# Where the conversion of the weights stands between softmax steps, and who swaps the halves of x: one start-up, two arrangements

## The chip, the core and the metric

The kernel runs on one core of a Trainium2 chip. The time is device microseconds from the first to the last instruction of the program on that core; the median of three runs is taken. The engines meant below are TensorE (PE in the profile, its weight loads PEld), VectorE (DVE), ScalarE (ACT), GpSimd (POOL, "Pool" in the text) and SyncE (SP), which here only issues transfers.

## The reference

Attention with a threshold, then a bilinear feed-forward network on its output. q, k and v have 8 batches, 8 heads, 576 rows and 64 columns, in float32; the three weights have 512 x 1536, 512 x 1536 and 1536 x 512 elements, in float64.

```python
scores = scale * np.matmul(q, k.transpose(0, 1, 3, 2))
thresh = np.max(scores, axis=-1, keepdims=True) - tau
scores = np.where(scores >= thresh, scores, -1000000000.0)
scores = scores - np.max(scores, axis=-1, keepdims=True)
attn = np.exp(scores)
attn = attn / (np.sum(attn, axis=-1, keepdims=True) + 1e-09)
attn_out = np.matmul(attn, v)
# bridge: (B,H,S,D) -> (B*S, H*D), 4608 x 512
x = attn_out.transpose(0, 2, 1, 3).reshape(B * S, H * D)
out = ((x @ w_a) * (x @ w_b)) @ w_out
```

## The kernel before

The attention goes by **units**: a pair of heads and 128 queries (units 0 to 3 of a pair), or the last 64 queries of both heads (unit 4, the *tail*). A unit's scores fill four 64 x 64 quadrants of TensorE, in float32. The feed-forward network goes by **blocks** of 256 rows of x; its steps are put between the units' steps by a budget of columns (`advance`), so that TensorE always has work once x and the weights are there. In the first units neither is there: x comes from the attention, and the weights come as float64 and are put together from their two 32-bit words by five small steps on three engines, one piece of 128 x 512 at a time, 36 pieces in all.

```python
def load_weights(limit, engine=nc.sync):
    while len(raws) < limit and state["loaded"] < NPIECES:
        n = state["loaded"]
        raw = work.tile([P, CW, 2], U32, tag="xT", bufs=XT_BUFS, name="raw")
        ...                                    # one or two transfers, 512 KB
        raws[n] = raw
        state["loaded"] = n + 1

def convert_first(n):                          # ScalarE, twice
    raw, top = raws[n], pieces[n][0]
    low = work.tile([P, CW], FP32, tag="osb", bufs=OSB_BUFS, name="low")
    nc.scalar.activation(top, raw[:, :, 1].bitcast(FP32), AF.Abs)
    nc.scalar.activation(low, raw[:, :, 0], AF.Copy, bias=2.0, scale=2.0 ** -51)
    stages[n] = low

def convert_clamp(n):                          # Pool
    nc.gpsimd.tensor_scalar(top, top, ..., op0=ALU.min, op1=ALU.max)

def convert_sign(n):                           # VectorE; gives the raw slot free
    nc.vector.scalar_tensor_tensor(out=low, in0=hi, scalar=0x80000000, in1=low,
                                   op0=ALU.bitwise_and, op1=ALU.bitwise_or)

def convert_shift(n):                          # VectorE
    nc.vector.tensor_scalar(top, top, 3, None, op0=ALU.logical_shift_left)

def convert_add(n):                            # Pool
    nc.gpsimd.tensor_tensor(top, top, low, op=ALU.add)
    state["converted"] = n + 1

def scores(i, u):
    ...
    for c in range(2):
        for t in range(n):                     # n = 2, in a tail 1
            for j in range(2):
                r = slice(j * D, (j + 1) * D)
                o = t if u < NT else 1 - j     # tails: crossed quadrants
                q0, to = (u * P + t * D if u < NT else MAIN), slice(o * D, (o + 1) * D)
                nc.tensor.matmul(sc[j if u < NT else 0][to, c], qT[r, q0:q0 + D],
                                 kT[r, c * SH:(c + 1) * SH], start=True, stop=True)
    ...                                        # VectorE: maxima; Pool: bias, threshold

def weigh(i, u):
    ...                                        # ScalarE: exponentials; VectorE: masks and sums

def turn_pe(i, u):                             # units 0 to 7: weights turned by TensorE
    tp = banks(512, "tp")
    ...                                        # 8 matmuls with diag(1 / sum)
    for j in range(2):
        nc.scalar.copy(wT[:, 5 * j:5 * j + NT], tp[:, j])
    tp = banks(P, "tp")[:, 0]
    ...                                        # 2 matmuls
    nc.scalar.copy(wT[:, NT], tp)

def exchange(x, xs, hp, c0, c1, engine):       # swaps the partition halves of x
    for r in range(2):
        engine.tensor_copy(xs[r * D:(r + 1) * D, hp, c0:c1], x[(1 - r) * D:(2 - r) * D, hp, c0:c1])

def weighted_unit(i, u):
    pv = product(turned.pop((i, u, "pe")), loaded[i]["v"], P)
    ...
    join(x_of[b, 0][:, hp, u * P:(u + 1) * P], pv[:, 0], pv[:, 1])
    exchange(x_of[b, 0], state["xs"], hp, u * P, (u + 1) * P, nc.vector)
    if hp == HP - 1:
        state["rows"] = u + 1
        if u == 0:
            blocks.append(((x_of[b, 0], state["xs"]), ("first", b, 0)))

def ffn(xT, what):
    n = CH // P                                # 2
    steps = [(f, 0, HALF) for f in range(NG * n)]
    if kind == "first":                        # the first block starts with half its rows
        steps = [(f, c, c + P) for c in (0, P) for f in range(n)] + steps[n:]
    ...
```

All PSUM tiles (scores, pv, tp, pab, po) come from one pool of four buffers of two banks each. Raw weights, x and xS share seven buffers. The loop over the units, cut to the conversion and the order around it (`of(g, False)` is the first piece of unit g, `of(g, True)` the others; units 0 to 3 have two pieces, 4 to 9 three, 10 to 14 two):

```python
for g in range(len(units) + PV_LAG):
    scores(i, u)
    ...
    if 2 <= g < BY_PE + 2:
        weighted_unit(*units[g - 2])
    for n in of(g - 1, False):
        convert_add(n)
    for n in of(g - 1, True):
        convert_clamp(n)
    if g < 3:
        prep_copy(*prep_pe(g + 1, "q"))        # VectorE: q and k of the next pair, turned
    for n in of(g - 1, True):
        convert_sign(n)
    load_weights(5 if g < 10 else 4)
    ...
    weigh(i, u)
    if 0 < g <= BY_PE:
        turn_pe(*units[g - 1])
    if g < 3:
        prep_copy(*prep_pe(g + 1, "k"))
    ...
    for n in of(g, False):
        convert_first(n)
        convert_clamp(n)
    reciprocal(i, u, ...)
    for n in of(g - 1, True):
        convert_shift(n)
    for n in of(g - 1, True):
        convert_add(n)
    ...                                        # diagonals or normalise, on ScalarE
    for n in of(g, False):
        convert_sign(n)
    load_weights(5 if g < 10 else 4)
    ...
    advance(...)                               # feed-forward steps
    for n in of(g, True):
        convert_first(n)
    for n in of(g, False):
        convert_shift(n)
    advance(PORTIONS[3] * pace)
```

Of the kernel before, what the change touches and what calls it, by code (L numbers as in the profile page):

```python
# [11 lines left out]
U32 = mybir.dt.uint32  # L12
# [38 lines left out]
def kernel(  # L51
# [11 lines left out]


# [118 lines left out]
    raws, stages = {}, {}  # L183
    state = {"loaded": 0, "converted": 0, "rows": 0}

    def load_weights(limit, engine=nc.sync):

        while len(raws) < limit and state["loaded"] < NPIECES:
            n = state["loaded"]
            raw = work.tile([P, CW, 2], U32, tag="xT", bufs=XT_BUFS, name="raw")  # L190
            src = pieces[n][1]
            for r, part in enumerate(src):
                dst = raw.rearrange("p f w -> p (f w)")[r * D:r * D + P // len(src)]
                if len(src) == 2:
                    dst = dst.rearrange("p (k f) -> p k f", k=2)
                engine.dma_start(dst, part)
            raws[n] = raw
            state["loaded"] = n + 1
# [37 lines left out]
    def convert_add(n):  # L236
        if n in stages:
            top, low = pieces[n][0].bitcast(I32), stages.pop(n).bitcast(I32)
            nc.gpsimd.tensor_tensor(top, top, low, op=ALU.add)
            state["converted"] = n + 1  # L240
# [4 lines left out]
    nc.sync.dma_start(tau_sb, tau.to_broadcast([P, 1]))  # L245
# [9 lines left out]
    load_rows(1, "k", rooms[3], nc.scalar)  # L255
    load_weights(2)
# [48 lines left out]
    def scores(i, u):  # L305
# [3 lines left out]
        for c in range(2):  # L309
            for t in range(n):  # L310
                for j in range(2):
                    r = slice(j * D, (j + 1) * D)
                    o = t if u < NT else 1 - j
                    q0, to = (u * P + t * D if u < NT else MAIN), slice(o * D, (o + 1) * D)
                    nc.tensor.matmul(sc[j if u < NT else 0][to, c], qT[r, q0:q0 + D],  # L315
                                     kT[r, c * SH:(c + 1) * SH], start=True, stop=True)
# [51 lines left out]
    def turn_pe(i, u):  # L368
# [16 lines left out]
        nc.scalar.copy(wT[:, NT], tp)  # L385
# [10 lines left out]
    def turn_blocks(i, u):  # L396
# [20 lines left out]
        else:  # L417
# [5 lines left out]
            for g in range(G):  # L423
                c = slice((1 - g // 2) * NB, (2 - g // 2) * NB)
                w0 = swap.shape[2] - TAIL + (g % 2) * Q
                nc.sync.dma_start(swap[c, :, w0:w0 + Q].rearrange("c p w -> p c w"),  # L426
                                  tb[g * Q:(g + 1) * Q])
# [43 lines left out]

    def weighted_unit(i, u):
# [7 lines left out]
        exchange(x_of[b, 0], state["xs"], hp, u * P, (u + 1) * P, nc.vector)  # L480
        if hp == HP - 1:
            state["rows"] = u + 1
            if u == 0:
                blocks.append(((x_of[b, 0], state["xs"]), ("first", b, 0)))
# [23 lines left out]
    def ffn(xT, what):  # L508
# [7 lines left out]
        if kind == "first":  # L516
            steps = [(f, c, c + P) for c in (0, P) for f in range(n)] + steps[n:]
# [115 lines left out]
    def of(g, late):  # L633

        return early.get(g, [])[1:] if late else early.get(g, [])[0:1]

    for g in range(len(units) + PV_LAG):
# [15 lines left out]
        for n in of(g - 1, False):  # L653
            convert_add(n)
        for n in of(g - 1, True):
            convert_clamp(n)
        if g < 3:
            prep_copy(*prep_pe(g + 1, "q"))
        for n in of(g - 1, True):
            convert_sign(n)  # L660
        load_weights(5 if g < 10 else 4)
# [21 lines left out]
        for n in of(g, False):  # L683
# [4 lines left out]
        for n in of(g - 1, True):  # L688
            convert_shift(n)
        for n in of(g - 1, True):  # L690
            convert_add(n)
# [4 lines left out]
        for n in of(g, False):  # L696
            convert_sign(n)
# [10 lines left out]
        for n in of(g, True):  # L708
            convert_first(n)
        for n in of(g, False):  # L710
            convert_shift(n)
# [38 lines left out]
```

## Time and profile before

| | before |
|---|---|
| median of 3 runs (lowest to highest) | 1526.21 us (1524.84 to 1528.06) |
| span of the profiled run, mean granted TensorE clock | 1524.0 us, 0.988 |
| busy: TensorE, weight loads | 1467.9 us (96%), 1145.1 us (75%) |
| busy: VectorE, ScalarE, Pool | 877.9 us (58%), 588.9 us (39%), 260.4 us (17%) |
| HBM read and written | 127.40 MB, 89.65 MB |
| raw weights | 36 pieces of 512 KB; median landing 4.2 to 5.4 us |

The page gives busy time as an average over the whole span, in which the first 165 us and the rest have different limits; so the views by stretches of time say more here. In the rows of groups the columns are: line, engine, operation, result<-inputs, shape, count | busy us, mean ns of one | idle time just before them, and what ended most of it. In the timeline they are: start, us, engine, line, operation, tiles, count, and in brackets the idle time before it and what ended it. TensorE shows two records for each float32 matmul.

### The profile page before, as it was taken

What the parts mean: (1) busy time and instruction counts of PE and PEld (TensorE: products, weight loads), DVE (VectorE), ACT (ScalarE), POOL (GpSimd) and SP (SyncE); (2) the same over time, 40 slices, a digit from 0 to 9 for tenths busy, and PEclk for the clock granted to TensorE, in tenths of its full rate; (3) what the DMA queues carried; (4) which work ended last, traced back from release to release, by engine and by line L of the source; (5) the groups of instructions that cost most, each with busy time, mean ns of one, the idle gap of its engine ahead of it and who ended that gap; (6) DMA issues with size and microseconds to landing.
All of it is one profiled execution on the core that took longest, in us unless ns stands there. A gap on an engine that the chain in (4) does not pass through costs nothing.

```text
span 1524.0 us, 51117 instructions
## 1 busy us (share of the span) xinstructions
PE 1467.9 (96%) x22640; PEld 1145.1 (75%) x22640; DVE 877.9 (58%) x1844; ACT 588.9 (39%) x935; POOL 260.4 (17%) x662
## 2 busy tenths in 40 slices
PE   5779999999999999999999999999999999999998
PEld 4567586786978587778877887778886978687775
DVE  4999677577756765665545755476655765610000
ACT  4667444344434443443333433344433443410000
POOL 2666311111110111121100101011110111110000
PEclk9889999999999999999999999999999999999999
DMA  9558888779867976796537966589648976530000
GB/s 196 134 154 210 184 149 204 167 165 189 202 150 160 188 188 134 157 184 153 138 93 143 194 147 144 115 180 186 154 112 162 189 175 128 127 79 15 2 16 15
DMA packets 624557, 220.38 MB, mean 145 GB/s; under 512 B 542928, under 2 KB 612048, under 8 KB 624336
## 3 DMA queue, kind: packets, MB, share of 16 engines
q1 hardware_dynamic: 621968, 216.52, 65.2%
q8 instruction: 178, 2.92, 0.8%
q10 hardware_dynamic: 2368, 0.59, 0.2%
q14 instruction: 43, 0.35, 0.1%
HBM read 127.40 MB, written 89.65 MB: 142 GB/s over the span
## 4 chain that ended last, share of the span: by engine, by line
PE 87%; DVE 6%; DMA 3%; SPq 1%; ACT 1%; issue 1%; POOL 0%; DVEq 0%; ACTq 0%; POOLq 0%
PE pab L533 45%; PE po L553 23%; PE pv L452 9%; PE sc L315 9%; DVE low L228 2%; DMA raw<-in_moe_w_a_dram 1%; DVE w L339 1%; DVE mx L322 1%; DVE tb L404 1%; DMA wT<-swap 0%; SPq L414 0%; SPq L426 0%; DVE wa_sb L234 0%; SPq L142 0%; DMA swap<-tb 0%
## 5 line engine op out<-in xcount | busy, mean ns | idle before, releaser
L553 PE MATMUL po<-wo_sb,h 64*64 64x512 f32 x3456 | 423.3, 590 | 0.0
L553 PEld LDWEIGHTS po<-wo_sb,h 64*64 64x64 f32 x3456 | 226.0, 133 | 130.3 <-issue 73.4
L322 DVE TENSOR_REDUCE mx<-sc 128x1 f32<-128x576 f32 x288 | 205.0, 749 | 201.6 <-PE sc L315 189.9
L335 ACT ACTIVATE w<-sc,bias,scalars 128x576 f32<-128x576 f32 x288 | 226.7, 827 | 188.7 <-POOL bias L323 180.9
L533 PE MATMUL pab<-xS,wa_sb 64*64 64x256 f32 (+1 forms) x3520 | 278.6, 373 | 3.3 <-POOL xS L462 3.3
L533 PE MATMUL pab<-xS,wb_sb 64*64 64x256 f32 (+1 forms) x3520 | 278.2, 375 | 0.5 <-issue 0.5
L315 PE MATMUL sc<-kT,qT 64*64 64x288 f32 x2304 | 254.4, 417 | 19.7 <-DVE w L339 8.4
L358 ACT ACTIVATE w<-w,rcp 128x576 f32<-128x576 f32 x272 | 197.7, 768 | 183.8 <-DVE rcp L352 183.7
L323 POOL TENSOR_SCALAR bias<-mx,scalars 128x1 f32<-128x1 f32 x288 | 84.8, 295 | 1032.0 <-DVE mx L322 617.4
L533 PE MATMUL pab<-xT,wb_sb 64*64 64x256 f32 (+1 forms) x3136 | 249.0, 374 | 1.7 <-DVE h L541 1.7
L533 PE MATMUL pab<-xT,wa_sb 64*64 64x256 f32 (+1 forms) x3136 | 246.2, 375 | 3.0 <-DVE xT L442 1.8
L339 DVE SCALAR_TENSOR_TENSOR w<-sc,thr,w 128x576 f32<-128x576 f32 x288 | 222.4, 804 | 18.7 <-ACT w L335 16.4
L533 PEld LDWEIGHTS pab<-xS,wa_sb 64*64 64x64 f32 x3520 | 193.5, 133 | 35.5 <-POOL xS L462 10.1
L533 PEld LDWEIGHTS pab<-xS,wb_sb 64*64 64x64 f32 x3520 | 197.0, 134 | 27.6 <-issue 1.1
L533 PEld LDWEIGHTS pab<-xT,wa_sb 64*64 64x64 f32 x3136 | 175.2, 134 | 28.9 <-DVE xT L442 2.1
L315 PEld LDWEIGHTS sc<-kT,qT 64*64 64x64 f32 x2304 | 148.0, 136 | 63.0 <-issue 20.1
L452 PE MATMUL pv<-wT,vm 64*64 64x320 f32 (+3 forms) x2592 | 192.8, 384 | 2.3 <-ACT h L539 1.4
L533 PEld LDWEIGHTS pab<-xT,wb_sb 64*64 64x64 f32 x3136 | 176.1, 134 | 24.2 <-DVE h L541 2.3
L404 DVE STREAM_TRANSPOSE tb<-w 128x576 f32<-128x576 f32 x240 | 171.4, 752 | 1.3 <-ACT w L358 1.3
L452 PEld LDWEIGHTS pv<-wT,vm 64*64 64x64 f32 x2592 | 149.2, 137 | 28.8 <-issue 8.1
L541 DVE TENSOR_TENSOR h<-h,pab 128x512 f32<-128x512 f32 (+1 forms) x110 | 72.8, 662 | 122.3 <-PE pab L533 121.7
L539 ACT COPY h<-pab 128x512 f32<-128x512 f32 (+1 forms) x110 | 63.1, 573 | 199.0 <-PE pab L533 198.5
(59 smaller groups left out, 744.4 us busy)
## 6 DMA issues: line engine op xcount, KB each, us to landing
swap<-tb SPq DMA_DIRECT2D x240, 288.0 KB, 5.3
wT<-swap SPq DMA_DIRECT2D x28, 1440.0 KB, 7.5
wT<-swap SPq DMA_DIRECT2D x32, 1152.0 KB, 6.3
vm<-in_v_dram SPq DMA_DIRECT2D x32, 288.0 KB, 4.9
swap<-tbt SPq DMA_DIRECT2D x128, 72.0 KB, 2.8
out_dram<-osb SPq DMA_DIRECT2D x32, 256.0 KB, 4.6
qm<-in_q_dram SPq DMA_DIRECT2D x112, 72.0 KB, 3.6
km<-in_k_dram SPq DMA_DIRECT2D x112, 72.0 KB, 4.8
```

Of the source, the lines that this page charges most:

```text
L315: nc.tensor.matmul(sc[j if u < NT else 0][to, c], qT[r, q0:q0 + D], kT[r, c * SH:(c + 1) * SH], start=True, stop=True)
L322: nc.vector.tensor_reduce(mx[:, c], sc[j], axis=AX.XY, op=ALU.max)
L323: nc.gpsimd.tensor_scalar(bias[:, c], mx[:, c], e_nscale, None, op0=ALU.mult)
L335: nc.scalar.activation(w.rearrange("p (c k) -> p c k", c=2), s, AF.Exp, bias=bias[:, j:j + 1], scale=e_scale)
L339: nc.vector.scalar_tensor_tensor(out=wv, in0=s, scalar=thr[:, j:j + 1], in1=wv, op0=ALU.is_ge, op1=ALU.mult, accum_out=sums[:, j:j + 1])
L358: nc.scalar.activation(w, w, AF.Copy, scale=rcp[:, j:j + 1])
L404: nc.vector.transpose(tb[:, j * NB:(j + 1) * NB, (u % 2) * Q:(u % 2 + 1) * Q], w.rearrange("p (n e) -> p n e", e=Q))
L452: nc.tensor.matmul(pv[j * D:(j + 1) * D, r], vm[rows, k0], wT[rows, k0], start=(s == (NT if j == r else 0)), stop=(s == NT - 1))
L533: nc.tensor.matmul(pab[c * D:(c + 1) * D, r], w[rows, f // n, k, fs + c * D:fs + (c + 1) * D], moving, start=(k == 0), stop=(k == H - 1))
L539: nc.scalar.copy(ht, pab)
L541: nc.vector.tensor_tensor(ht, ht, pab, op=ALU.mult)
L553: nc.tensor.matmul(po[c * D:(c + 1) * D, r], ht[rows, t0:t0 + D], wo_sb[rows, F, :], start=(F == 0), stop=(F == NF - 1))
```

## The change

VectorE and Pool are to stop getting in each other's way while the weights are converted. In each unit, all signs and then all shifts of the pieces of the unit before now stand on VectorE between maxima and masks; Pool's additions stand behind the last shift, the last piece's first. The two halves of x of the first eight units are swapped by transfers from SyncE's queue instead of copies on VectorE, after the second of the two places where raw weights could be asked for. Four more raw slots come, once, from the buffers that later hold turned weights (tag tb). The small copy of wT goes from ScalarE to VectorE. The first block takes four column groups instead of two by half its rows. tau is loaded after the first rows of q and k. And the tails' scores use the straight quadrants, (0,0) and (1,1), where before they used the crossed ones.

```diff
-        while len(raws) < limit and state["loaded"] < NPIECES:
+        while (len(raws) < limit or extra) and state["loaded"] < NPIECES:
             n = state["loaded"]
-            raw = work.tile([P, CW, 2], U32, tag="xT", bufs=XT_BUFS, name="raw")
+            if len(raws) < limit:
+                raw = work.tile([P, CW, 2], U32, tag="xT", bufs=XT_BUFS, name="raw")
+            else:
+                raw = extra.pop(0)
...
-    nc.sync.dma_start(tau_sb, tau.to_broadcast([P, 1]))
...
     load_rows(1, "k", rooms[3], nc.scalar)
+    nc.sync.dma_start(tau_sb, tau.to_broadcast([P, 1]))
...
-                    o = t if u < NT else 1 - j
-                    q0, to = (u * P + t * D if u < NT else MAIN), slice(o * D, (o + 1) * D)
+                    q0, to = (u * P + t * D, slice(t * D, (t + 1) * D)) if u < NT else (MAIN, r)
...
-        nc.scalar.copy(wT[:, NT], tp)
+        nc.vector.tensor_copy(wT[:, NT], tp)
...
-                c = slice((1 - g // 2) * NB, (2 - g // 2) * NB)
+                c = slice(g // 2 * NB, (g // 2 + 1) * NB)
...
+    def exchange_dma():
+        while exchanges:
+            x, xs, hp, c0, c1 = exchanges.pop(0)
+            for r in range(2):
+                nc.sync.dma_start(xs[r * D:(r + 1) * D, hp, c0:c1], x[(1 - r) * D:(2 - r) * D, hp, c0:c1])
+            if hp == HP - 1:
+                state["rows"] = c1 // P
+                if c0 == 0:
+                    blocks.append(((x, xs), ("first", 0, 0)))
...
-        exchange(x_of[b, 0], state["xs"], hp, u * P, (u + 1) * P, nc.vector)
-        if hp == HP - 1:
-            ...
+        exchanges.append((x_of[b, 0], state["xs"], hp, u * P, (u + 1) * P))
...
-            steps = [(f, c, c + P) for c in (0, P) for f in range(n)] + steps[n:]
+            steps = [(f, c, c + P) for c in (0, P) for f in range(2 * n)] + steps[2 * n:]
...
-        for n in of(g - 1, False):
-            convert_add(n)
-        for n in of(g - 1, True):
-            convert_clamp(n)
         if g < 3:
             prep_copy(*prep_pe(g + 1, "q"))
-        for n in of(g - 1, True):
+        for n in early.get(g - 1, []):
             convert_sign(n)
+        for n in early.get(g - 1, []):
+            convert_shift(n)
+        for n in early.get(g - 1, [])[-1:] + early.get(g - 1, [])[:-1]:
+            convert_add(n)
+        if g == 3:
+            ...                                # two tb buffers give four raw slots: extra
         load_weights(5 if g < 10 else 4)
...
-        for n in of(g, False):
+        for n in early.get(g, [])[:1]:
             convert_first(n)
             convert_clamp(n)
         if here:
             reciprocal(i, u, nc.scalar if converting else nc.vector)
-        for n in of(g - 1, True):
-            convert_shift(n)
-        for n in of(g - 1, True):
-            convert_add(n)
         ...                                    # diagonals or normalise
-        for n in of(g, False):
-            convert_sign(n)
+        for n in early.get(g, [])[1:]:
+            convert_first(n)
+            convert_clamp(n)
+        exchange_dma()
         load_weights(5 if g < 10 else 4)
...
-        for n in of(g, True):
-            convert_first(n)
-        for n in of(g, False):
-            convert_shift(n)
```

## The prediction

> **What bounds the kernel now.** I read the page's slices first, to see where TensorE isn't full.
>
> ```profile
> PE   5779999999999999999999999999999999999998
> DVE  4999677577756765665545755476655765610000
> ...
> PEclk9889999999999999999999999999999999999999
> ```
>
> A slice is 38 us. TensorE is full from the fourth on, and its waits from 165 us to the end sum to 7 us. The end is therefore set by how much TensorE work is done in the first 165 us. There VectorE is the fullest engine. The second view is the windows by unit: I cut the stretch where each unit's first maximum starts (28.5, 42.9, 52.9, 60.9, 71.3, 83.1, 95.0, 105.4, 117.2 us for units 2 to 10, then 127.1, 134.8, 142.6, 151.9, 159.5, and 167.3 for unit 16).
>
> ```profile
> core 0: us, PE busy (x) PEld busy (x) DVE busy (x) ACT busy (x) POOL busy (x), PEclk, DMA share, GB/s
> 28.50:42.90 14.40, 7.81 (x92) 5.91 (x86) 8.31 (x17) 6.20 (x13) 4.92 (x7) 0.74 0.83 162
> ...
> 71.30:83.07 11.77, 8.99 (x144) 7.97 (x148) 10.10 (x18) 7.12 (x14) 7.80 (x9) 0.71 0.58 137
> ...
> 134.81:142.57 7.76, 7.72 (x136) 5.80 (x132) 7.76 (x16) 6.13 (x11) 5.28 (x7) 1.00 1.03 334
> ```
>
> A unit takes 10 to 12 us while three pieces of weights are converted beside it, VectorE is busy for 10 of them, and the granted clock falls to 0.71. Third, VectorE's groups from 0 to 165 us, then the timeline of one unit:
>
> ```profile
> L228 DVE SCALAR_TENSOR_TENSOR low<-raw,low 128x512 uint32<-128x512 uint32 x36 | 38.6, 1084 | 0.2
> ...
> L234 DVE TENSOR_SCALAR wa_sb<-wa_sb 128x512 uint32<-128x512 uint32 x12 | 11.2, 933 | 0.0
> ...
> L462 DVE COPY xS<-xT 64x128 f32<-64x128 f32 x16 | 4.8, 302 | 5.2 <-DMA raw<-in_moe_w_a_dram 4.8
> ```
>
> ```profile
> 67.85 0.42 DVE L234 TENSOR_SCALAR wa_sb<-wa_sb 128x512 uint32<-128x512 uint32 x1
> 68.02 1.39 POOL L239 TENSOR_TENSOR wb_sb<-wb_sb,low 128x512 int32<-128x512 int32 x1 [1.27 <-DVE wb_sb L234]
> 68.19 1.77 DVE L228 SCALAR_TENSOR_TENSOR low<-raw,low 128x512 uint32<-128x512 uint32 x1
> ```
>
> A sign step (L228) takes 0.68 us alone (58.83 us) and 1.77 us beside a Pool addition. A shift (L234) takes 0.42 alone and 1.5 beside one. The masks (L339) take 0.80 each beside a Pool clamp at 56.6 us, as everywhere. Of the 36 sign steps 36 x (1.084 - 0.68) = 14.5 us is waiting, of the 35 shifts (28.9 us in their three groups) 28.9 - 35 x 0.42 = 14.2 us.
>
> **What the Trainium skill says.** "SBUF — State Buffer", section "Who interferes with whom", says that VectorE and GpSimd share a port pair as an exclusive lock, taken by a Vector instruction with two SBUF inputs or in a two-port mode, and not by one with at most one SBUF input or by a reduction. The trace agrees: signs (two SBUF inputs) and shifts stretch by 1.1 us, masks (one input in PSUM) don't. "TensorE: Matmul & The Clock Gate", Part 1, says that idling lowers the clock and work restores it: the trace has 0.71 here and 1.00 later. "TensorEngine Tiling (Array Packing)", "Key Properties", says that tiles operate independently; the tail lines below agree.
>
> **The change part by part.**
>
> *Placement of the conversion.* In each unit VectorE now does its 2 or 3 signs and shifts together between maxima and masks, and Pool adds only after the last shift, hence beside masks, the next maxima and waits. Pool's additions (1.27) and clamps (0.61) fit between: 3 x 1.27 + 3 x 0.61 = 5.6 us after the masks begin. Some 29 us of VectorE's waiting should go.
>
> *Exchange by transfers.* 16 copies leave VectorE, 4.8 us, and a stall of 4.8 us before the first (36.27 us). The program's order shows what that stall is: xS lies in the slot of unit 3's k rows and must wait until TensorE has transposed them, at 36.2 us. This wait moves to the SyncE queue. A transfer is 32 KB; the 72 KB transfers of tbt land after a median of 2.8 us. They queue behind up to six pieces of 512 KB, but TensorE needs the first four only in unit 5.
>
> *The 128-column copy of wT* goes from ScalarE to VectorE: 8 x 0.28 = 2.2 us more there; ScalarE no longer stands in line for TensorE and the mask there.
>
> *More half-width steps.* Four instead of two column groups of the first block run 128 wide. Full-clock records start 0.87 us apart per 32 at 128 columns (65.61 to 66.48 us) and 1.73 at 256 (202.21 to 203.94), so the split is nearly free. It gives TensorE 264 instead of 220 of these instructions before unit 10: 44 x 2 records x 0.027 = 2.4 us of work earlier.
>
> *Four spare slots* for raw weights from unit 3 on, out of the later tb buffers: they fill gaps in the transfers (DMA share 0.6), no direct gain.
>
> *The tails' quadrants.* 32 score units of 64 queries use the straight instead of the crossed quadrants.
>
> ```profile
> 614.07 0.41 PE L315 MATMUL sc<-kT,qT 64*64 64x288 f32 x2
> 614.09 0.64 PE L553 MATMUL po<-wo_sb,h 64*64 64x512 f32 x1
> 614.32 0.65 PE L315 MATMUL sc<-kT,qT 64*64 64x288 f32 x4
> 614.57 0.65 PE L553 MATMUL po<-wo_sb,h 64*64 64x512 f32 x2
> 614.80 0.41 PE L315 MATMUL sc<-kT,qT 64*64 64x288 f32 x2
> 615.00 1.93 PE L553 MATMUL po<-wo_sb,h 64*64 64x512 f32 x16
> ```
>
> A tail takes 0.93 us of the output stream, in which three output records of 0.109 us (55 in the 6.0 us before) start: it costs 0.60 us, where 8 records at the pace of a full unit (16 records in 0.97 us, 199.95 to 200.92) would be 0.49. The instruction behind it goes to quadrant (0,0), which crossed tails leave free. Straight ones occupy it, so I expect the two other quadrants to start only at the half: two idle half-spans instead of one, 0.5 us of one quadrant, 0.125 us a tail, 32 x 0.125 = +4 us. That is an inference from start times, my least certain term.
>
> **The sum, by units.** VectorE's work in a unit with three pieces becomes 1.33 (maxima) + 0.27 (join) + 3 x 0.60 + 3 x 0.34 (start to start) + 1.49 (masks) + 0.28 + 0.1 + 0.33 = 6.6 us, from 10. ScalarE, with the timeline's durations: 1.55 (exponentials) + 1.07 (wT) + 3 x 1.16 (conversion) + 0.2 + 0.69 + 0.35 + 0.25 = 7.6. TensorE: 0.97 (scores) + 36 x 0.027 (pv) + 2.4 (turn) + 44 x 2 x 0.027 (first block) = 6.8. None of these is the period: the next scores need the banks that masks, wT copies or h copies free. Followed through the new order: from a unit's first maximum to the end of its masks 5.9 us (0.67 + 0.67 + 0.27 + 1.8 + 1.0 + 1.5), then most of the first-block matmuls (about 2 us), the scores (1.0) and a bank that waits for ScalarE's h copy in unit 7: 9 to 10.5 us. I take 9.5, 9.0, 10.5, 9.2 and 9.5 for units 5 to 9 (before: 10.4, 11.8, 11.9, 10.4, 11.8), 8.0 and 7.7 for 3 and 4 (before 9.95 and 8.0), and 10.0 for unit 2 (before 14.4). Together 73.4 after 28.5 us: unit 10's maximum at 101.9 instead of 117.2, **-15.3 us**. More work done by then: **-2.4**. Units 10 to 15 take 50.1 us, of which VectorE has 7 to 10 each; TensorE idles 4.7 us in them (50.1 less the 45.4 of the windows) and waits at half speed for more; I take **-3**. Tails **+4**. Sum -16.7: 1526.2 - 16.7 = 1509.5, say **1510 us**.
>
> **Rivals.** *VectorE alone sets the start:* then its 29 + 4.8 + 4.8 - 2.2 = 36 us all come off: 1490 us. For it speaks that the windows have it busy for 94% of 50 to 160 us; against it, that TensorE's scores end at 82.7 us where VectorE takes the maximum at 83.07, so TensorE and the banks are right behind. *ScalarE or the weight transfers take over:* ScalarE has 7.6 us in a unit plus waits for banks, and the third piece's slot is given free only when the signs of the unit before are done, while landing takes 4.2 to 5.4 us; if each of units 4 to 9 stays at 10.5 us, what remains is unit 2's stall, some 6 us in the early units, less the tails: about 1522 us. *Tails worse than estimated:* if they find no overlap, each costs 0.93 instead of 0.60, +10.6 us in place of +4: about 1516 us.
>
> **Range and chances.** The start cannot shrink much below what units 10 to 15 show without three pieces, and each rival moves the time by 6 to 20 us: 1497 to 1522. A gain of 2% needs 1495.7, which takes the VectorE rival nearly whole and harmless tails: 0.09. Over 2% slower needs a new stall of 47 us: 0.02. Within: 0.89.
>
> **What would show it.** Signs at 0.68 and shifts at 0.42 in the groups, no stall at xS, unit 10's first maximum near 102 us, TensorE's waits in the first 165 us fallen, granted clock nearer 1; a tail between output records at about 0.73 us net. Wrong would be: signs still over 1 us (Pool's additions have slid into them), the units at 8 us or at 11, TensorE waiting for xS transfers in unit 5, or the stretch after unit 16 differing by more than the tails' 4 us.

## The result, and the profile after

| | before | after |
|---|---|---|
| median of four runs (lowest to highest) | 1525.8 us (1524.8 to 1528.1) | 1534.2 us (1532.9 to 1535.9) |
| ratio, 95% interval | | 1.0053 (1.0036 to 1.0071) |
| profiled span | 1524.0 us | 1534.1 us |
| start: until unit 16's first maximum | 167.2 us | 158.7 us |
| the rest, from there to the end | 1356.8 us | 1375.4 us |
| busy: TensorE | 1467.9 us | 1479.0 us |
| busy: VectorE | 877.9 us | 848.6 us |

The changed kernel is 8 us slower, where 16 us of gain were predicted. The two lower parts of the table say where to look: the start is 8.5 us shorter, and the stretch behind it, in which only the tails' quadrants differ, is 18.6 us longer. The work left for it is the same: counted in the two traces, 6.294 and 6.296 million columns (a record streams 64 to 512 columns through its quadrant). The slices of the page after:

```profile
PE   5778999999999999999999999999999999999998
DVE  5667576666656765674545754576555764510010
...
PEclk9999999999999999999999999999999999999999
```

TensorE is full from the fifth slice on, and VectorE, which stood at 9 from the second to the fourth, no longer does: the change did what it was made for. Next, the groups of 0 to 165 us, first VectorE's, then Pool's (mean ns of one behind the comma):

```profile
L229 DVE SCALAR_TENSOR_TENSOR low<-raw,low 128x512 uint32<-128x512 uint32 x32 | 20.7, 688 | 1.5 <-ACT low L217 1.5
...
L235 DVE TENSOR_SCALAR wa_sb<-wa_sb 128x512 uint32<-128x512 uint32 x12 | 5.0, 418 | 0.0
```

```profile
L323 POOL TENSOR_SCALAR bias<-mx,scalars 128x1 f32<-128x1 f32 x33 | 17.1, 559 | 27.7 <-DVE mx L322 27.5 <-POOL wb_sb L223 0.2
...
L324 POOL TENSOR_SCALAR thr<-mx,scalars 128x2 f32<-128x2 f32 (+1 forms) x17 | 12.1, 710 | 0.0
```

Signs take 0.69 us instead of 1.08, and the shifts of w_a 0.42 instead of 0.93 (those of all three weights 0.83 in the mean before). The lock has turned round: Pool's bias and threshold, 0.37 and 0.30 us in the same stretch before, now take 0.56 and 0.71, where they run beside signs and shifts.

The windows by unit, cut at each unit's first maximum (units 2, 5, 7, 9 and 14 shown; columns as in the windows of the prediction):

```profile
27.89:36.38 8.49, 6.07 (x93) 4.81 (x88) 6.66 (x15) 5.87 (x14) 4.53 (x7) 1.00 1.11 229
...
48.45:63.32 14.87, 10.69 (x176) 9.16 (x169) 6.38 (x15) 10.28 (x21) 10.22 (x13) 0.79 0.94 208
...
72.68:83.65 10.97, 7.79 (x172) 6.48 (x167) 6.80 (x16) 7.80 (x16) 8.29 (x11) 1.00 0.47 103
...
92.67:105.71 13.04, 9.04 (x230) 8.07 (x234) 8.24 (x18) 8.04 (x17) 6.82 (x10) 0.87 0.49 163
...
141.62:149.23 7.61, 3.94 (x71) 2.74 (x67) 6.25 (x15) 5.91 (x10) 5.37 (x7) 1.00 0.75 247
```

Unit 2 has lost its stall (8.5 us, from 14.4) and unit 7 takes 11.0 us, where 10.5 were expected; but units 5 and 9 take 14.9 and 13.0 us. In unit 14 TensorE is idle for 3.7 us though VectorE is busy for only 6.3 of 7.6. And the windows of the whole rest, before and after, in the same columns:

```profile
167.18:1524.00 1356.82, 1344.29 (x20762) 1047.25 (x20754) 740.73 (x1599) 487.61 (x742) 166.84 (x537) 1.00 0.65 141
```

```profile
158.69:1534.10 1375.41, 1363.50 (x20766) 1024.54 (x20758) 741.69 (x1598) 488.61 (x742) 165.69 (x536) 1.00 0.64 139
```

TensorE is idle for 11.9 us of 1375.4, no more than before (12.5 of 1356.8), at full clock and with the same work (20766 and 20762 records). It does the same records more slowly. That is what the first experiments are about.

### The profile page after: what moved, and what is told of

Read it like the earlier page. It is cut to its first block, busy times and chain, and to the rows that moved or that the text cites. A ratio compares the mean times of both kernels' runs of the same rounds, so it can differ in the third digit from the quotient of the medians.

```text
span 1534.1 us, 51632 instructions
## 1 busy us (share of the span) xinstructions
PE 1479.0 (96%) x22896; PEld 1116.3 (73%) x22896; DVE 848.6 (55%) x1838; ACT 588.1 (38%) x929; POOL 260.7 (17%) x662
## 4 chain that ended last, share of the span: by engine, by line
PE 89%; DVE 3%; DMA 2%; ACT 2%; SPq 1%; issue 1%; POOL 1%; DVEq 0%; POOLq 0%; ACTq 0%
PE pab L541 46%; PE po L561 23%; PE sc L315 9%; PE pv L452 9%; PE tp L377 1%; DVE mx L322 1%; DVE tb L404 1%; SPq L414 1%; SPq L426 0%; DMA wT<-swap 0%; ACT low L217 0%; SPq L140 0%; DVE low L229 0%; DMA swap<-tb 0%; DMA raw<-in_moe_w_a_dram 0%
## 5 line engine op out<-in xcount | busy, mean ns | idle before, releaser
L315 PE MATMUL sc<-kT,qT 64*64 64x288 f32 x2304 | 261.1, 411 | 16.4 <-DVE kT L304 7.7
L323 POOL TENSOR_SCALAR bias<-mx,scalars 128x1 f32<-128x1 f32 x288 | 89.8, 317 | 1041.3 <-DVE mx L322 625.2
L541 PEld LDWEIGHTS pab<-xS,wa_sb 64*64 64x64 f32 x3584 | 188.6, 133 | 40.2 <-POOL xS L462 9.7
L541 PEld LDWEIGHTS pab<-xS,wb_sb 64*64 64x64 f32 x3584 | 190.9, 134 | 29.6 <-issue 1.0
L541 PEld LDWEIGHTS pab<-xT,wb_sb 64*64 64x64 f32 x3200 | 169.5, 134 | 32.1 <-DVE h L549 4.3
L541 PEld LDWEIGHTS pab<-xT,wa_sb 64*64 64x64 f32 x3200 | 167.1, 133 | 33.7 <-issue 3.1
L452 PE MATMUL pv<-wT,vm 64*64 64x320 f32 (+3 forms) x2592 | 184.5, 380 | 5.3 <-ACT h L547 2.8
L452 PEld LDWEIGHTS pv<-wT,vm 64*64 64x64 f32 x2592 | 132.3, 133 | 46.8 <-issue 9.2
L549 DVE TENSOR_TENSOR h<-h,pab 128x512 f32<-128x512 f32 (+1 forms) x112 | 73.2, 654 | 132.5 <-PE pab L541 128.6
```

Of the source, the lines that this page charges most:

```text
L323: nc.gpsimd.tensor_scalar(bias[:, c], mx[:, c], e_nscale, None, op0=ALU.mult)
L452: nc.tensor.matmul(pv[j * D:(j + 1) * D, r], vm[rows, k0], wT[rows, k0], start=(s == (NT if j == r else 0)), stop=(s == NT - 1))
L541: nc.tensor.matmul(pab[c * D:(c + 1) * D, r], w[rows, f // n, k, fs + c * D:fs + (c + 1) * D], moving, start=(k == 0), stop=(k == H - 1))
L549: nc.vector.tensor_tensor(ht, ht, pab, op=ALU.mult)
```

## Experiments on the rest: which quadrants go together

**How the loss at one event is measured.** In a steady stream 32 records of 256 columns start in 1.73 us, 0.211 ns a column. I take the time from 0.8 us before the first record of a tail or a pv product to 1.6 us after its last, and subtract 0.2115 ns for each column started in it. What remains is TensorE's time lost there. A record at the window's edge counts whole or not at all, 0.05 us at 256 columns and 0.11 at 512, so one event's figure is good to about 0.1 us, and the sums and the whole times carry the argument. A tail puts 8 records of 288 columns on two quadrants of four; with nothing beside them on the other two it loses what its columns would take in a full stream, 8 x 288 x 0.2115 ns = 0.49 us. A pv product (the weights of a unit times v) has 36 records, and its half slot (the step over the last 64 keys of each head, `NT`) puts 4 of them on the straight quadrants (0,0) and (1,1): by the same working at most 0.22 us lost at 256 columns and 0.27 at 320.

From the traces of before and after, 170 to 1340 us: the tails with what stands within 1.2 us of them lose 6.1 us before and 14.7 after, the other pv products 5.1 and 12.1. So the pv products, which the change does not touch, lose 7 us more as well; together that is 15.6 of the 18.6 us. In the kernel before most products behind a tail cost nothing (-0.03 us), and three in a row without a tail between them cost 0.16, 0.19 and, with the tail behind it, 0.2. In the kernel after most of them cost 0.15 to 0.3. Theory, "balance": two quadrants that were left behind stay behind, and the next event that loads only the other two then costs nothing. Crossed tails and straight half slots fill each other; straight and straight don't. Rival: straight tails are bad by themselves, because the next instruction goes to quadrant (0,0), and the rest comes from elsewhere in the change.

**a_cross**, the change with crossed tails:

```diff
-  (...) if u < NT else (MAIN, r)
+  (...) if u < NT else (MAIN, slice((1 - j) * D, (2 - j) * D))
-                c = slice(g // 2 * NB, (g // 2 + 1) * NB)
+                c = slice((1 - g // 2) * NB, (2 - g // 2) * NB)
```

> The changed kernel with the tails' scores back on the crossed quadrants, everything else as changed. Theory 'balance': a tail and the half slot that begins each pv product each load only two of the four quadrants; on different pairs (crossed tail, straight pv) the one fills what the other left empty, on the same pair both are paid in full. From the two traces that is 8.7 us at the tails and 7.0 us at the pv products, some 17 us in all with what lies around them: 1517 us (1515 to 1519). Rival 'tails alone': only the tails' own 9 us come back and the rest has another cause in the change: 1525 us. Rival 'something else in the later stretch': 1534 us, unchanged.

**b_straight**, the kernel before with straight tails:

```diff
-  o = t if u < NT else 1 - j
+  o = t if u < NT else j
-  c = slice((1 - g // 2) * NB, (2 - g // 2) * NB)
+  c = slice(g // 2 * NB, (g // 2 + 1) * NB)
```

> The kernel before with the tails' scores on the straight quadrants, nothing else changed. Balance: 1526 + 17 = 1543 us. Tails alone: 1535 us. Something else: 1526 us.

**a_pvx**, the change with straight tails and crossed half slots:

```diff
-  nc.tensor.matmul(pv[j * D:(j + 1) * D, r], vm[rows, k0], ...
+  nc.tensor.matmul(pv[(1 - j) * D:(2 - j) * D, r], vm[rows, k0], ...
-  w[rows, f // n, k, fs + c * D:...], moving,
+  w[rows, f // n, (k + HP) % H, fs + c * D:...], moving,
```

> The changed kernel, tails straight, but every pv product writes each head to the other half of the partitions, so that its half slot lies on the crossed quadrants (the feed-forward reads the weights' chunks in the swapped order, the result is the same). Balance: a straight tail and a crossed half slot fill each other again, 1518 us (1515 to 1521). Rival 'straight is worse than crossed wherever it stands' (the instruction behind goes to quadrant (0,0)): the tails keep their loss of 0.45 us and the 60 pv products gain about 0.1 us each, 1528 us. Something else: 1534 us.

**b_pvx**, the same two edits in the kernel before:

> The kernel before, tails crossed, with the pv products' half slots crossed too. Balance: both now lean on the same pair, and the pv products behind a tail pay the 0.2 to 0.25 us that they did not pay before, 32 x 0.25 = 8 us: 1534 us (1530 to 1538). Rival 'straight is worse wherever it stands': 1520 us. Something else: 1526 us.

| run | tails | half slots | ratio to before (95%) | rest, us | lost at tails | lost at other pv |
|---|---|---|---|---|---|---|
| before | crossed | straight | 1 | 1356.8 | 6.1 | 5.1 |
| a_cross | crossed | straight | 0.9968 (0.9956 to 0.9980) | 1358.4 | 5.8 | 4.2 |
| a_pvx | straight | crossed | 0.9962 (0.9950 to 0.9974) | 1361.1 | 6.9 | 6.3 |
| after | straight | straight | 1.0053 (1.0036 to 1.0071) | 1375.4 | 14.7 | 12.1 |
| b_straight | straight | straight | 1.0125 (1.0110 to 1.0140) | 1373.9 | 15.2 | 11.5 |
| b_pvx | crossed | crossed | 1.0118 (1.0103 to 1.0133) | 1375.2 | 12.3 | 13.2 |

"Rest" is the window from unit 16's first maximum to the end of each profile; the losses are sums in us. The line of a_pvx, to be read beside that of after above:

```profile
160.59:1521.70 1361.11, 1349.54 (x20766) 1003.04 (x20758) 741.24 (x1600) 488.57 (x742) 165.58 (x536) 1.00 0.64 141
```

14 us less than after, with the tails still straight, and as a whole 1520.1 us like a_cross: no quadrant pair is worse than the other, and it isn't the instruction behind that counts. What counts is whether both kinds of event lean on the same pair. b_straight came out at 1542.8 us (1543 expected). The rival falls at both ends: it had a_pvx at 1528 us (1520.1 measured) and b_pvx at 1520 us (1542.2 measured). My own figure for b_pvx, 1534, was too low by 8 us: there the tails lose more too (12.3 us instead of 6.1), as they would if the half slots had already used up what the crossed quadrants could lag. In a_cross the medians moved by 14 us instead of the 17 expected, and the rest by 17.0 (1375.4 to 1358.4).

The timeline of before shows the lag. A tail at 636.39 us, and the change from xT to xS behind it (start, us, engine, line, operation, tiles, count):

```profile
635.49 1.24 PE L533 MATMUL pab<-xT,wa_sb 64*64 64x256 f32 x15
636.39 0.41 PE L315 MATMUL sc<-kT,qT 64*64 64x288 f32 x2
...
637.38 0.43 PE L533 MATMUL pab<-xS,wa_sb 64*64 64x256 f32 x1
637.58 0.44 PE L533 MATMUL pab<-xT,wa_sb 64*64 64x256 f32 x3
...
638.01 0.38 PE L533 MATMUL pab<-xT,wa_sb 64*64 64x256 f32 x2
638.07 1.46 PE L533 MATMUL pab<-xS,wa_sb 64*64 64x256 f32 x21
```

The first xS record starts at 637.38 while xT records go on starting until past 638.01, although the program has all xT instructions ahead of all xS ones. The profile doesn't say on which quadrant a record runs; I read it so that two quadrants are already at the next tile while the other two, which had the tail, work off the one before. The same overlap of 0.6 us is still there at the last change of tile ahead of the pv product at 648.76, with a full unit of scores in between (643.0 to 644.9 us):

```profile
647.03 0.38 PE L533 MATMUL pab<-xT,wb_sb 64*64 64x256 f32 x1
...
647.61 0.38 PE L533 MATMUL pab<-xS,wa_sb 64*64 64x256 f32 x2
```

The same tail in the kernel after:

```profile
635.50 1.19 PE L541 MATMUL pab<-xT,wa_sb 64*64 64x256 f32 x14
636.52 0.89 PE L315 MATMUL sc<-kT,qT 64*64 64x288 f32 x5
...
637.98 0.38 PE L541 MATMUL pab<-xS,wa_sb 64*64 64x256 f32 x2
638.14 0.38 PE L541 MATMUL pab<-xT,wa_sb 64*64 64x256 f32 x2
638.20 1.83 PE L541 MATMUL pab<-xS,wa_sb 64*64 64x256 f32 x28
```

Here the first five records of the tail start with nothing between them, the hand-over from xT to xS is a tight two and two, within 0.2 us, and the quadrants end level. By the measure above this tail costs 0.47 us and that of before 0.21; and nothing is left that a half slot could fill, so the pv product at 649.7 us pays 0.24 us, where that at 648.8 before pays -0.03.

**a_alt** and **b_alt** use this on purpose: of the pv products in a row without a tail between them, the first (hp 0 of the first half) goes to the crossed quadrants, in a_cross and in the kernel before.

```diff
+  flip = int(h == 0 and hp == 0)              # product(..., flip): j ^ flip in the output half
+  (k + HP) % H if kind == "half" and h == 0 and k % HP == 0 else k      # index of the weights' chunk
```

> The changed kernel with crossed tails (1520 us), and of the four pv products in a row that have no tail between them the first of each group written with its half slot on the crossed quadrants (the feed-forward reads those chunks of the weights in swapped order, the result is the same). Balance: the flipped product and the straight one behind it cancel, each 0.15 to 0.19 us now, about 0.3 us in each of 7 groups, 2 us: 1518 us, and in the trace these two products at about 0 us each. Rival (only a tail right beside a product helps): no change at these products, 1520 us.

> The kernel before, with only the first pv product of each untailed row of four turned to the crossed quadrants. Balance: two products in each of 7 groups lose their 0.15 to 0.19 us, about 2 us in all, ratio 0.9985 (1523.5 us for 1525.8). Rival: no change, ratio 1.000.

In both traces the two products cost -0.02 us each instead of 0.16 and 0.19 (at 876 and 894 us in b_alt), and the third with its tail 0.07 to 0.13 instead of 0.2. b_alt: ratio 0.9980 (0.9970 to 0.9990), 1522.7 us, and the rest falls from 1356.8 to 1354.5 us. a_alt: 0.9956 (0.9943 to 0.9969), 1518.8 us, which a_cross's interval overlaps; its profiled run has two stalls of 4.2 us together that the profile puts to no cause, so its span says nothing of the 2 us. The rival (only a tail right beside helps) falls.

## Experiments on the start

All on a_cross or on the kernel before. The time of one and the same kernel spreads here by 5 to 10 us from run to run (a_cross 1516.1 to 1525.0), and the clock granted in the start differs as well: unit 5 ran at 0.79 in the profile of after and at 1.00 in that of a_cross. The start itself spreads too. Its code is the same up to the tails in after, a_cross, a_pvx and a_alt, and unit 10's first maximum stands at 105.7, 102.3, 107.6 and 107.5 us in their profiles; in those of before, b_straight, b_pvx and b_alt it stands at 117.2, 116.7, 113.3 and 113.8. So I read ratios to the kernel before, timed anew beside each group of runs, and one profile's units only for their mechanism.

First the two units that were mispredicted. TensorE's timeline in unit 5 of the kernel after:

```profile
54.43 1.10 PE L541 MATMUL pab<-xT,wa_sb 64*64 64x128 f32 x32 [2.12 <-POOL thr L324]
...
56.96 1.36 PE L541 MATMUL pab<-xS,wa_sb 64*64 64x128 f32 x16 [1.21 <-DMA xS<-xT]
58.78 0.86 PE L541 MATMUL pab<-xS,wa_sb 64*64 64x128 f32 x8 [0.47 <-DMA xS<-xT]
...
60.97 2.30 PE L315 MATMUL sc<-kT,qT 64*64 64x288 f32 x16
```

This is where the first block begins: 95 more TensorE records than in the unit before (176 against 81), which all stand ahead of the next scores in the queue. The first waits for its bank, which held tp until ScalarE's second copy of wT ended at 54.33 (the profile names Pool; by the program's order of the banks it waits for that copy); then TensorE stands twice at xS. Four experiments:

**a_xact**, xS asked for from ScalarE's queue:

```diff
-  nc.sync.dma_start(xs[r * D:(r + 1) * D, hp, c0:c1], ...
+  nc.scalar.dma_start(xs[r * D:(r + 1) * D, hp, c0:c1], ...
```

> The changed kernel with crossed tails (1520 us), and the exchange of x issued from ScalarE's queue instead of SyncE's, in the same place. Theory 'queue': in unit 5 TensorE stands at xS because its transfers were asked for late, behind SyncE's waits for raw slots; asked for earlier, unit 5 falls from 12.5 us to about 10 and the whole by 2.5 us, to 1517.5 us. Rival 'traffic': the small transfers take 5 us because the pieces fill the DMA engines, whichever queue asks; unit 5 stays at 12 to 13 us, the whole at 1520 us.

Ratio 1.0003 (0.9990 to 1.0016): 5 us worse than a_cross, not better. TensorE's waits from 46 to 75 us of this run (us in total, times, longest):

```profile
PE pab L541 <- DMA xS<-xT: 5.9, 1, 5.9
```

Its last transfers of unit 3 were asked for at 62.2 us and let TensorE go at 68.5. SyncE, which no longer stood at xS, had asked for five pieces between 55.2 and 63 us; unit 5 takes 19.7 us here. That the transfers took 6.2 us on the other queue speaks for the traffic. But ScalarE asked for these last ones no earlier than SyncE had: 8.3 and 8.9 us after the unit's first maximum, where SyncE asked between 6.9 and 8.1 us in a_cross. What asking earlier would bring was not tried.

**a_copy**, the exchange by VectorE's copies in the same place (behind the masks):

```diff
-  nc.sync.dma_start(xs[...], x[...])
+  exchange(x, xs, hp, c0, c1, nc.vector)
```

> The changed kernel with crossed tails (1520 us), and the exchange of x by copies on VectorE, in the place where the transfers are asked for. If the transfers' landing holds unit 5 up and VectorE has room: unit 5 at 10 us, the whole at 1518 us. If VectorE is still the bound of the units: its 4.8 us of copies come on top, unit 5 gains nothing net, 1524 us.

0.9953 (0.9936 to 0.9970), 1520.0 us, between the two figures; unit 5 takes 11.4 us (54.07 to 65.47) instead of 12.5. The transfers bring nothing that late copies don't; the interval overlaps that of a_cross.

**a_narrow**, two column groups of the first block by half its rows, as before:

```diff
-  ... for f in range(2 * n)] + steps[2 * n:]
+  ... for f in range(n)] + steps[n:]
```

> The changed kernel with crossed tails (1520 us), and the first block with two column groups by half its rows, as before, instead of four. By the prediction's step (the other 44 instructions are work done earlier, the split nearly free): 1522.5 us. Rival: each narrow step costs its copy and product on ScalarE and VectorE, and those stand in the units' chain: 1517 us.

0.9954 (0.9935 to 0.9972), 1519.2 us, between the two figures: the four groups bring no gain that can be seen.

**a_clamp**, Pool's later clamps behind the next unit's bias and threshold:

```diff
   for n in early.get(g, [])[1:]:
       convert_first(n)
-      convert_clamp(n)
   ...
+  for n in early.get(g - 1, [])[1:]:
+      convert_clamp(n)
   for n in early.get(g - 1, []):
       convert_sign(n)
```

> The changed kernel with crossed tails (1520 us), and Pool's clamps of a unit's later pieces put behind the next unit's bias and threshold instead of ahead of them. Theory: in units 10 to 15 Pool's bias waits behind a clamp that waits for ScalarE, so the exponentials start up to 2 us late; without it these six units, 53.5 us together, lose 4 to 6 us and the whole falls to 1516 us. Rival: the exponentials aren't on the path there (TensorE waits for h copies), 1520 us.

0.9998 (0.9988 to 1.0007): it costs 4 to 5 us, and units 10 to 15 take 59.0 us instead of 53.5. VectorE's waits, 107 to 167 us of this run:

```profile
DVE wo_sb L235 <- POOL wo_sb L223: 3.8, 5, 0.8
```

The shift needs the clamp, and everything on VectorE stands behind the shift: one wait was exchanged for another.

Unit 9 in a_cross (VectorE, ScalarE's h copy and TensorE):

```profile
94.98 0.37 ACT L547 COPY h<-pab 128x256 f32<-128x256 f32 x1 [0.96 <-PE pab L541]
...
95.27 0.42 DVE L235 TENSOR_SCALAR wa_sb<-wa_sb 128x512 uint32<-128x512 uint32 x1
95.61 1.44 DVE L404 STREAM_TRANSPOSE tb<-w 128x576 f32<-128x576 f32 x2
...
96.96 0.39 DVE L549 TENSOR_TENSOR h<-h,pab 128x256 f32<-128x256 f32 x1
...
97.40 1.99 PE L541 MATMUL pab<-xT,wb_sb 64*64 64x128 f32 x32 [2.49 <-DVE h L549]
```

ScalarE copied h out of a bank at 94.98, as soon as TensorE had filled it. TensorE's next bank is freed by VectorE's product (L549); its inputs were there since 92.9 us, but it came only at 96.96, behind the signs, the shifts and two transposes. TensorE stood 2.5 us. The batch of the conversion is cheap in itself, but what TensorE needs from VectorE now stands behind all of it.

Then the parts, one against the others:

**a_late**, the pieces of units 10 on in the order of before; **a_late0**, the same for all units; **a_place**, nothing but the new order, VectorE's small copy, late copies of x and tau's later load (a_cross with the edits of a_copy and a_narrow, and no spare slots).

```diff
+  LATE = 10                                  # a_late; 0 in a_late0
+  # pieces of g >= LATE: additions, clamps, signs and shifts in the places of before (of(g, late))
-  for n in early.get(g - 1, []):             # sign, shift, add
+  for n in (early.get(g - 1, []) if g - 1 < LATE else []):
```

```diff
-  if g == 3:                                 # a_place: no spare slots
+  if False:
```

> The changed kernel with crossed tails (1520 us), and the pieces of units 10 on converted in the order of before; units 0 to 9 keep the new order. Theory: with two pieces in a unit the new order costs more than it gives, since signs and shifts stand on VectorE ahead of the transposes, the h products and the masks that TensorE waits for; units 10 to 15 fall from 53.5 us to the 50 us of before, the whole to 1516.5 us. Rival: what unit 10 begins with (late banks, late pieces) sets their length, the order doesn't matter: 1520 us.

> The changed kernel with crossed tails (1520 us), and the conversion in the order of before in all units; transfers of x, spare slots, four column groups and VectorE's small copy stay. Theory: the order carries nearly all of the start's gain of 9 to 11 us: without it 1529 us (VectorE has the small copy in addition). Rival: the other parts carry it: 1520 us.

> The changed kernel with crossed tails (1520 us), without its transfers of x (copies on VectorE behind the masks), without the spare slots, with two narrow column groups: what is left is the order of the conversion and the small copy. Theory: the order alone gives the start's gain, 1518 to 1521 us. Rival: the parts need each other (no slots, no early pieces), 1525 us or more.

**b_xlate**, the kernel before with its copies of x behind the masks; **b_xlwt**, the same with VectorE's small copy of wT:

```diff
-  exchange(x_of[b, 0], state["xs"], hp, u * P, (u + 1) * P, nc.vector)
+  exchanges.append(...)          # done by VectorE behind the unit's masks
-  nc.scalar.copy(wT[:, NT], tp)                # b_xlwt alone
+  nc.vector.tensor_copy(wT[:, NT], tp)
```

> The kernel before with one change: VectorE's copies of x of the first eight units stand behind the unit's masks instead of ahead of its exponentials. Theory 'one stall': in unit 2 VectorE stood 4.8 us at these copies with everything behind it; all variants of the change have taken that away, and nothing else in them moves the start, so this alone gives 1519 to 1521 us. Rival 'any one of several parts is enough only together with another': 1524 us or more.

> As the kernel before with its copies of x behind the masks, and the small copy of wT on VectorE instead of ScalarE. If the small copy frees TensorE earlier: 2 to 3 us below the run with late copies alone, about 1517 us. If VectorE is short: 1 to 2 us above it.

**b_noconv**, the kernel before without signs, shifts and additions (its weights are only magnitudes, clamped):

```diff
-  nc.vector.scalar_tensor_tensor(out=low, in0=hi, scalar=0x80000000, ...)
-  nc.vector.tensor_scalar(top, top, 3, None, op0=ALU.logical_shift_left)
-  nc.gpsimd.tensor_tensor(top, top, low, op=ALU.add)
```

> The kernel before without the signs, shifts and Pool additions of the weights' conversion (the weights stay unconverted but for magnitude and clamp; nothing else is left out). It measures how much of the start VectorE and Pool hold at all. By the prediction's working (28.7 us of waits on VectorE are what stretches the units): with 67.5 us of VectorE's work gone the start shrinks by at least 20 us, 1505 us or less. Theory 'a chain through TensorE, ScalarE and the banks is close behind': 1514 to 1519 us.

| run | ratio to before (95%) | unit 10's first maximum, us | units 10 to 15, us |
|---|---|---|---|
| before | 1 | 117.2 | 50.0 |
| after | 1.0053 (tails straight) | 105.7 | 53.0 |
| a_cross | 0.9968 (0.9956 to 0.9980) | 102.3 | 53.5 |
| a_late | 0.9955 (0.9938 to 0.9972) | 105.4 | 51.0 |
| a_late0 | 0.9969 (0.9955 to 0.9983) | 104.3 | 54.7 |
| a_place | 0.9943 (0.9921 to 0.9965) | 104.3 | 52.4 |
| b_xlate | 1.0013 (0.9992 to 1.0033) | 114.9 | 51.8 |
| b_xlwt | 0.9995 (0.9978 to 1.0011) | 112.1 | 52.0 |
| b_noconv | 0.9817 (0.9792 to 0.9841) | 90.3 | 45.2 |

Three things follow. The stall in unit 2 was worth nothing in the end: b_xlate shortens that unit to 10.5 us (13 to 14.4 in the four profiles of the old start), and the whole gains nothing; my 1519 to 1521 us was wrong (1527.3 measured). b_xlwt lies 2.5 us below b_xlate, intervals overlapping. The order alone is worth some 8 us: a_place against b_xlwt, which has the same late and small copies, 0.9943 against 0.9995, intervals apart; a_place's 1518.2 us is the figure expected. The other parts on the old order are worth some 4 us (a_late0 against b_xlwt, intervals overlapping), and on top of the new order nothing (a_cross against a_place). Nor does the order bring anything once the other parts are there: a_late0 came out at 1521.2 us, the figure of its rival and not my 1529, and its ratio is a_cross's, 0.9969 against 0.9968. Order and other parts don't add; which wait they share stays open. a_late, at 1518.8 us, lies between its two figures. And b_noconv bounds it all: with the 67.5 us of signs and shifts gone from VectorE (38.6 and 28.9 in the kernel before), and Pool's additions, the whole gains 29 us. Windows of that run, units 5 and 7:

```profile
46.54:57.64 11.10, 9.09 (x177) 8.26 (x181) 3.86 (x12) 8.46 (x19) 2.64 (x6) 0.85 0.88 213
...
66.02:74.41 8.39, 7.00 (x156) 5.64 (x150) 4.83 (x12) 7.14 (x17) 2.61 (x6) 1.00 0.83 192
```

With VectorE busy for 3.9 and 4.8 us in them, units 5 and 7 still take 11.1 and 8.4 us: other work stands right behind VectorE. ScalarE is busy for 8.5 and 7.1 us of them and TensorE for 9.1 and 7.0; which hand-over between them sets the length was not tried. Of the two figures expected the prediction's, 1505 us or less, holds, and the chain's, 1514 to 1519, falls: at 1496.4 us VectorE's work does count. But it counts at most 29 / 67.5 = 0.43 us for each us of it (Pool's additions are gone as well); the prediction had 20.7 us for 28.7 + 4.8 us of waits, 0.62 for each.

**a_best** and **a_best2** join parts: a_place with the turned product of a_alt, and (a_best only) the late order of a_late.

> Parts joined: the changed kernel with crossed tails, the first pv product of each untailed row of four on the crossed quadrants, copies of x on VectorE behind the masks, two narrow column groups, no spare slots, and the pieces of units 10 on converted in the order of before. If the gains add: 1518 (order alone) less 2 (quadrants) less 1 to 2 (late order): 1514.5 us. If the start's parts don't add: 1516 us.

> The order of the conversion and the small copy on VectorE, crossed tails, copies of x on VectorE behind the masks, two narrow column groups, no spare slots (0.9943 of before), and the same turned products. If the 2 us add: ratio 0.993, 1515.5 us. If not: 0.9945, 1518 us.

a_best: 0.9949 (0.9932 to 0.9965), 1517.7 us; the gains of the start don't add. a_best2: 0.9930 (0.9907 to 0.9954), 1517.4 us: faster than both kernels by 0.7% and 1.2%, with an interval that also holds a_place alone.

## Why the prediction was wrong, by its own steps

1. **The waits between VectorE and Pool.** Right: signs 0.69 us (0.68 said), shifts 0.42 (0.42 said), together 36 x (1.084 - 0.689) + 35 x (0.829 - 0.418) = 28.6 us of waiting gone (28.7 said). That agrees with "SBUF — State Buffer", "Who interferes with whom" of the Trainium skill. I had not counted its other side, that section's remark that the order of issue decides who blocks: Pool's bias and threshold now wait.
2. **Units 2 to 4.** 25.7 us said, 20.6 measured: better than said.
3. **Units 5 to 9.** 9.5, 9.0, 10.5, 9.2 and 9.5 said; 14.9, 9.4, 11.0, 9.0 and 13.0 measured (12.5 and 12.9 in a_cross for the first and last), 47.7 us against 57.3. The step that failed is to treat 5 and 9 as units like the others. Unit 5 is where the first block starts; even b_noconv needs 11.1 us for it. I had taken the landing of transfers of x from tbt's median of 2.8 us; it was 5.3 (4.4 in a_cross), and TensorE stood 1.7 us at xS in unit 5, one of the signs of being wrong that the prediction names. In unit 9 the first transposes of the other path come in, and the h product stands behind the batch. So unit 10's maximum came at 105.7 us instead of 101.9. The 102.3 of a_cross is from the fastest of its fifteen runs; a_pvx and a_alt, with the same start, have 107.6 and 107.5.
4. **Units 10 to 15**, "TensorE idles 4.7 us in them and waits at half speed for more; I take -3". 47.1 us said, 53.0 measured, slower than before. This step of the start failed. b_noconv needs 45.2 us for these units: my 47.1 was nearly a unit without conversion on VectorE. TensorE's idle time in them rose from 4.7 us to 10.1 (six windows: 53.0 less 42.9 busy). Its waits went from one busy engine to several hand-overs: before, 4.6 us for masks; in a_cross, 4.7 us for ScalarE's h copies, 2.9 for VectorE's h products and 1.6 for masks. a_late, with the old order there, has 51.0 us, but a_late0, with the old order everywhere, 54.7, and the four profiles of the new start 52.8 to 53.5: which hand-over sets these six units stays open.
5. **More work of the first block by then, -2.4.** a_narrow takes it away and loses nothing: the term falls. At unit 10's first maximum the first block was indeed 6912 columns further than before, 1.5 us of work at 0.2115 ns; at unit 16's, where the end is set, the two kernels had started equally many.
6. **The tails, +4.** The largest miss: +17 us (1356.8 to 1373.9 in b_straight, whose start is as before). I had called it my least certain term, and the rival "if they find no overlap", +10.6, had its local part: it said 0.33 us a tail, and the tails lost 8.6 us more, 0.3 us each. What neither had is the other 7 us at the pv products. The step that failed is to reckon a tail's cost from the one instruction behind it, and not from where the next imbalance comes, 12 us later. The Trainium skill, "TensorEngine Tiling (Array Packing)", "Key Properties", says that tiles operate independently; the traces agree, and show that it reaches much further than one instruction.

The sum: 8.5 us won in the start instead of 20.7, and 18.6 lost in the rest instead of 4, in the two profiles. Over the four profiles with either start, unit 16's first maximum comes at 164.4 to 167.2 us before and at 155.9 to 160.6 after, 7 us earlier in the mean. In whole times the new start is worth 4.9 us with crossed tails (a_cross against before) and 11 us with straight ones (after against b_straight); why the two differ stays open. So even with harmless tails about half or less of the 20.7 us came. The rival "VectorE alone, 1490 us" is refuted by b_noconv, which takes away nearly twice that work and reaches 1496. The check named at the end, the stretch after unit 16 differing by more than the tails' 4 us, is the one that gave the cause away.

## What to carry to other kernels

When instructions on part of TensorE's array stand in a full stream, add up what each quadrant gets over ten microseconds and more, and set the odd ones of successive steps on opposite quadrants: here that is worth 17 us of 1525 and costs nothing. The waits of one busy engine are worth only the distance to the chain behind it; before counting them as time, take that engine's work out altogether (here 67.5 us of work, and Pool's additions with it: 29 us of time). And when work is gathered into a batch, look at what the bound engine needs from behind the batch.

## What the runs showed of the hardware

- A lead of one pair of quadrants over the other lasts: the lag of a crossed tail at 636.4 us was still there, 12 us and some 200 records later, for the half slot at 648.8. It was used up where the next event leaned the other way, and a full unit of scores in between (which uses all four) left it alone.
- Matmuls on different quadrants do not start in the program's order: xS records at 637.38 before xT records at 637.58. The Trainium skill, "TensorE: Matmul & The Clock Gate", Part 3, has them start and end in program order; here the measurement decides otherwise for the starts on 64x64 quadrants. Of the ends these profiles say nothing, since they are modelled.
- 32 KB transfers between two tiles of SBUF took 5.3 us to land (median, 40 to 70 us of after; 4.4 in a_cross), and 6.4 us when ScalarE's queue asked for them while SyncE asked for five pieces of weights (median, 45 to 75 us of a_xact).
